# Left operands 64 bytes off x's places, second matrix all decoded in the first product's stage, attention's tail planned by arrival

## The chip, the cores and the metric

The kernel runs on one core of a Trainium2 chip. Its time is device time in microseconds. Places in time are measured from the start of the profiled span.

## What is computed

Softcapped attention without a mask, then a two-layer block with a squared ReLU. Only the lines that compute are kept:

```python
# q, k, v: (4, 12, 448, 64) float32; w_in: (768, 2048), w_out: (2048, 768) as 64-bit floats
scores = cap * np.tanh(np.matmul(q, k.transpose(0, 1, 3, 2)) / np.sqrt(64) / cap)
attn = np.exp(scores - scores.max(-1, keepdims=True))
attn = attn / (attn.sum(-1, keepdims=True) + 1e-09)
x = np.matmul(attn, v).transpose(0, 2, 1, 3).reshape(1792, 768)
h = np.maximum(x @ w_in, 0.0)
return (h * h @ w_out).astype(np.float32)
```

The two matrices come as 64-bit floats, so the kernel fetches their raw words and turns them into 32-bit values itself. This is called decoding here.

## The kernel before

The core works in three stages.

**Attention**, about 0 to 177 us. 24 pairs of heads (`n`), one iteration of the loop each (`for n in range(NP + 1)`). PE does the scores (L389, L397), ACT the tanh and the exponential (L407, L415), PE the sums (L440) and the product with v (L431, L434, L447). DVE transposes q and k, adds, copies the two results out of PSUM (`take_sums`, `evac`), inverts the sums (`invert`, L464 and L465) and multiplies (`normalise`, L487). Between `invert` and `normalise` the reciprocals go to DRAM and come back spread over the partitions, by two DMAs that POOL issues (`spread`, L475). Six halves of `w_in` are decoded in the gaps.

**First product**, about 177 to 390 us: x @ w_in by Strassen's scheme. x is kept as four blocks `x11`, `x12`, `x21`, `x22`, and each block and each left operand is split in a high and a low part, so that one product is three matmuls for each of three chunks (L337). Four units with the blocks themselves ("u") come first, then seven products of two times nine matmuls for each pair `p` of 128 columns of w_in (`seq`, L664). Sums of blocks, `t1` to `t4` (`minus`, L742; `t1` = `x12` − `x11`), and their splits (`split_x`: ACT's high part L717, DVE's low part L723) are made at the beginning of this stage. Left operands come from decoded halves of `w_in` (`round_pair`, `other_ops`, `split_w`), and the results go through ReLU to `g_dram`. In the same stage halves of `w_out` are decoded (`part`) and stored to `w_dram`. A half costs ACT two steps (L39, L42) and DVE four (L40, L43, L45, L47).

The order of this stage is written by a planner (`Plan`). Each task has an engine, a cost, what it comes after with a lag, a due time, at times an earliest start (`ready`) and a buffer token. The planner goes through time, gives each engine the task that can start first and, among those, the one due first, and emits the instructions in that order. On the chip each engine then works through its queue in this order and waits where something has not arrived. The planner's time 0 is some 173 us of the span, and its `END` is 204.5. A half of `w_out` may not be fetched more than 16 before its due time (`round_half(..., early)`), and the due times lie evenly between `WSTART` and `END - WEND`.

**Second product**, 390 us to the end: relu² @ w_out, also by Strassen, in 49 products of 24 matmuls (L1096) in the order of `PRODUCTS`. The loop variable `z` counts them. In step z the raw `a` for product z + 5 is loaded from `g_dram` (L992) and the one of z + 4 squared on ACT (L996). The left operand of product z + 2 is split into `gh` (ACT, L1085) and `gl` (DVE, L1086), and `weights(z)` makes the right operands `th`, `tl`, two 1536-column halves at a time (L1180, L1184, L1185). Three pairs of buffers hold left operands, two in the pool `opp` on the right side of SBUF and one in `opp2` on the left. In this stage before the change the last eight halves of `w_out` are fetched and decoded in steps 0 to 8 (`fetch_half`, `round_half_to`).

**Places in SBUF.** Pools are laid one after another from the left (`lctx`, `rctx`, `actx`, `mctx`) and from the right. A pool that is opened over closed ones waits until those are done with as a whole, unless it has `reuse_waits="tile"`. In the layout of the kernel before, the pools `xab`, `w` (tiles `op`), `xf`, `xg0`, `xg1`, `xg2` all begin 32 bytes past a multiple of 128, and all their tiles are multiples of 128 long. In the second product `th` and `tl` lie at 32; `gh` and `gl` lie at 96, in `opp2` because of the pool `opad` (48 words) in front of it, and in `opp` because the right-hand end of the space lies at 96. `opp2` lies over `ep`, where the tiles `u`, `e`, `es`, `rb` were, and `scr` and `scr2`, with the decode's tiles, are on the right.

Of the kernel before, what the change touches and what calls it, by code (L numbers as in the profile page):

```python
# [239 lines left out]
def tile_softcap_attention_mlp(ctx, tc, q, k, v, cap, w_in, w_out, out):  # L240
# [18 lines left out]
    NRAW = 7  # L259
    LEAD = 5  # L260
    WSTART, WEND = 65.0, 15.0
# [7 lines left out]
    sctx = ctx.enter_context(ExitStack())  # L269
    actx = ctx.enter_context(ExitStack())  # L270
    xab = lctx.enter_context(tc.tile_pool(name="xab", bufs=NQ))
    wpool = rctx.enter_context(tc.tile_pool(name="w", bufs=8))
    xf = rctx.enter_context(tc.tile_pool(name="xf", bufs=2 * NQ))
    tmp = rctx.enter_context(tc.tile_pool(name="tmp", bufs=3))
    ep = rctx.enter_context(tc.tile_pool(name="ep", bufs=2))
    ps_s = rctx.enter_context(tc.tile_pool(name="ps_s", bufs=3, space=PSUM))

    hpad = actx.enter_context(tc.tile_pool(name="hpad", bufs=1))
    hpad.tile([P, 112], F32, name="hpad")
    qp = actx.enter_context(tc.tile_pool(name="qp", bufs=4))  # L280
    scr = sctx.enter_context(tc.tile_pool(name="scr", bufs=1, side="right"))
# [30 lines left out]
    def fetch_w(pool, f, o, first, bufs, tag="wraw"):  # L312
        raw = pool.tile([P, HO], U64, tag=tag, name="wraw", bufs=bufs)
# [182 lines left out]

    E = mybir.EngineType
# [76 lines left out]
    for n in range(NP + 1):  # L574
# [50 lines left out]
        if old:  # L625
            evac(n - 1)

    make_identity(nc, ident)
    for _ in decoding:
# [8 lines left out]
    xg = [c.enter_context(tc.tile_pool(name=f"xg{i}", bufs=NHALF, reuse_waits="tile"))  # L638
          for i, c in enumerate((rctx, tctx, tctx))]
    scr2 = sctx.enter_context(tc.tile_pool(name="scr2", bufs=1, side="right", reuse_waits="tile"))  # L640
# [211 lines left out]
    t1 = [minus(at + c, x11[c], x12[c], x11[c]) for c in range(NHALF)]  # L852
# [125 lines left out]
    quads = [(f, o) for o in range(2) for f in range(NF) if f < HF or not o]  # L978
# [11 lines left out]
    def load_a(tt, k):  # L990
        t = later["raw"].tile([P, HF, P], F32, tag="a", name="a")
# [29 lines left out]
    def move():  # L1021
        tctx.close()
        sctx.close()
        for name, bufs in (("opp", 2), ("raw", NRAW), ("tb", 2)):
            later[name] = lctx.enter_context(tc.tile_pool(name=name, bufs=bufs, side="right", reuse_waits="tile"))
# [3 lines left out]
    b21 = [None, None]  # L1029

    def load_b21(g):
        b21[g] = later["tb"].tile([P, HG * HO], F32, tag="t", name="tr")
        nc.sync.dma_start(out=b21[g], in_=w_dram[1, 0, g])

# [26 lines left out]
    for g in range(2):  # L1061
        do("SP", 0.35, partial(load_b21, g), moved, *stores[1, 0], lag=6.0, due=END - 8.0 + g)
# [4 lines left out]
    with ExitStack() as mctx:  # L1067
        mctx.enter_context(tc.manual_schedule(engines={E.PE, E.Activation, E.DVE, E.SP}))
        ps_o2 = mctx.enter_context(tc.tile_pool(name="ps_o2", bufs=6, space=PSUM))
        tw2 = mctx.enter_context(tc.tile_pool(name="tw2", bufs=12))  # L1070
        mctx.enter_context(tc.tile_pool(name="opad", bufs=1)).tile([P, 48], F32, name="opad")
        opp2 = mctx.enter_context(tc.tile_pool(name="opp2", bufs=1))
        ob = mctx.enter_context(tc.tile_pool(name="ob", bufs=3))
        sv = mctx.enter_context(tc.tile_pool(name="sv", bufs=2 * HT))
# [86 lines left out]
        def fetch_t():  # L1161
            tr[0] = [new_t(tw2, F32) for _ in range(2)]
            for g in range(2):
                nc.sync.dma_start(out=tr[0][g], in_=w_dram[0, 1, g])

        halves = {}

        def fetch_half(k):
            if k == 0:
# [106 lines left out]
```

## Time and profile before

| | us |
|---|---|
| median of 3 runs | 607.47 |
| lowest, highest | 606.35, 607.81 |
| the profiled execution, its own time | 608.97 |
| its span, first to last instruction | 607.40 |
| PE busy in the span | 586.2 |
| attention / first product / second product, about | 177 / 213 / 213 |

The profile is one execution. Its table by stage gives the busy time of each engine in each stretch, the granted clock of PE as a share of 2.4 GHz, the mean busy share of the DMA engines, and GB/s. The timeline gives start, length, engine and line, and in brackets how long the engine had stood idle before it and what released it. "x36" stands for 36 instructions in a row. Matmuls overlap, so a run of n matmuls is measured from its start to the start of the next run.

### The profile page before, as it was taken

To read this page: it belongs to the slowest core of one execution; us is meant where nothing else is said; L and a number is where in the kernel's file an instruction comes from. 1 tells how busy PE (TensorE), PEld (TensorE's weight loads), DVE (VectorE), ACT (ScalarE), POOL (GpSimd) and SP (SyncE) were. 2 spreads that over 40 slices of the span, in tenths; PEclk is the share of its full clock that TensorE was granted. 3 is DMA by queue.
4 is the path that set the end of the run, shared out by engine and by line. 5 is a ranking of instruction groups with operands and counts; after the bars stand their busy time and mean duration, and the time that the engine had idled before them with its cause. 6 is when DMAs were issued, how large, how long until landed. Compare 5 with 4: busy or idle time off the path is not lost. (4 is left out here: it accounts for less than half of the span.)

```text
span 607.4 us, 9533 instructions
## 1 busy us (share of the span) xinstructions
PE 586.2 (97%) x3286; PEld 459.2 (76%) x3286; DVE 488.4 (80%) x787; ACT 418.8 (69%) x564; POOL 125.3 (21%) x197
## 2 busy tenths in 40 slices
PE   8999999999999899999999999979999999999996
PEld 5333333333368789999989999869999899999996
DVE  2879999999868998898988885349999998766751
ACT  5998889999953676676767665659778965454430
POOL 8687788775310000000000000000000000000000
PEclk9999999999999999999999999989999999999999
DMA  9999797595424316788776885978599616656611
GB/s 132 140 169 173 142 161 149 129 161 125 104 53 135 114 56 210 218 259 250 239 240 206 250 257 195 339 258 262 163 260 307 187 36 196 190 159 167 178 39 43
DMA packets 149270, 107.04 MB, mean 176 GB/s; under 512 B 54528, under 2 KB 139776, under 8 KB 149216
## 3 DMA queue, kind: packets, MB, share of 16 engines
q1 hardware_dynamic: 140032, 89.69, 55.3%
q0 software_dynamic: 7648, 16.41, 13.7%
q8 instruction: 27, 0.44, 0.3%
q10 hardware_dynamic: 1536, 0.27, 0.3%
q14 instruction: 27, 0.22, 0.2%
HBM read 81.27 MB, written 24.99 MB: 175 GB/s over the span
## 5 line engine op out<-in xcount | busy, mean ns | idle before, releaser
L1096 PE MATMUL po<-th,gh 128*128 128x384 f32 x728 | 190.6, 337 | 4.0 <-ACT gh L1085 4.0
L1096 PEld LDWEIGHTS po<-th,gh 128*128 128x128 f32 x728 | 132.5, 189 | 4.4 <-ACT gh L1085 4.4
L1096 PE MATMUL po<-th,gl 128*128 128x384 f32 x392 | 132.6, 338 | 1.8 <-DVE gl L1086 1.8
L337 PE MATMUL hps<-xt,op 128*128 128x448 f32 x450 | 94.7, 367 | 0.3 <-DVE xt L723 0.3
L1085 ACT CAST gh<-a 128x1024 fp32r<-128x1024 f32 x47 | 49.3, 1048 | 61.5 <-PE po L1096 46.1
L337 PEld LDWEIGHTS hps<-xt,op 128*128 128x128 f32 x450 | 84.3, 188 | 8.2 <-DVE xt L723 0.7
L407 ACT ACTIVATE p<-sc 128x896 f32<-128x896 f32 x84 | 73.1, 909 | 17.4 <-PE sc L389 17.3
L1096 PEld LDWEIGHTS po<-th,gl 128*128 128x128 f32 x392 | 74.1, 189 | 3.1 <-DVE gl L1086 3.1
L415 ACT ACTIVATE p<-p 128x1792 f32<-128x1792 f32 (+1 forms) x48 | 72.5, 1510 | 1.3
L337 PE MATMUL hps<-xs,op 128*128 128x448 f32 x324 | 69.4, 368 | 2.7 <-ACT hps L932 2.7
L1086 DVE TENSOR_TENSOR gl<-a,gh 128x1024 fp32r<-128x1024 f32 x47 | 57.3, 1219 | 14.0 <-ACT gh L1085 14.0
L337 PEld LDWEIGHTS hps<-xs,op 128*128 128x128 f32 x324 | 60.3, 188 | 10.5 <-ACT hps L932 4.0
L996 ACT ACTIVATE a<-a 128x1024 f32<-128x1024 f32 x56 | 57.9, 1054 | 9.3 <-DMA a<-g_dram 9.1
L389 PE MATMUL sc<-kq 64*128 64x448 f32 x288 | 60.7, 554 | 0.0
L447 PE MATMUL pa<-p,vn 128*64 128x448 f32 x288 | 59.4, 548 | 0.0
L346 POOL DMA_DIRECT2D kqn<-in_k_dram x92 | 58.6, 643 | 3.6 <-issue 1.7
L337 PE MATMUL hps<-xh,op 128*128 128x448 f32 x168 | 50.5, 367 | 1.2 <-ACT u L942 1.2
L389 PEld LDWEIGHTS sc<-kq 64*128 64x128 f32 x288 | 25.7, 186 | 34.0 <-issue 24.1
L42 ACT ACTIVATE rest<-wraw 128x384 uint32<-128x384 uint32 x64 | 35.3, 552 | 10.6 <-DVE wf L47 10.6
L447 PEld LDWEIGHTS pa<-p,vn 128*64 128x64 f32 x288 | 18.5, 136 | 30.9 <-issue 30.9
L371 POOL DMA_DIRECT2D vn<-in_v_dram x48 | 35.3, 740 | 31.9 <-PE pa L447 23.6
L47 DVE CUSTOM_DVE_ANT_0 wf<-wf,rest 128x768 uint16<-128x768 uint16 x56 | 30.9, 552 | 6.8 <-ACT rest L42 2.3
(95 smaller groups left out, 839.2 us busy)
## 6 DMA issues: line engine op xcount, KB each, us to landing
a<-g_dram SPq DMA_DIRECT2D x56, 512.0 KB
wraw<-in_moe_w_in_dram SPq DMA_DIRECT2D x32, 384.0 KB
wraw<-in_moe_w_out_dram SPq DMA_DIRECT2D x32, 384.0 KB
g_dram<-r SPq DMA_DIRECT2D x36, 224.0 KB
g_dram<-u SPq DMA_DIRECT2D x28, 224.0 KB
vn<-in_v_dram POOLq DMA_DIRECT2D x48, 112.0 KB, 4.6
rb<-rd POOLq DMA_DIRECT2D x48, 112.0 KB, 3.5
kqn<-in_q_dram SPq DMA_DIRECT2D x93, 56.0 KB
```

What stands on the lines that cost most here:

```text
L42: rest=lambda rest: nc.scalar.activation(out=rest, in_=low, func=ACTF.Copy, scale=2.0 ** -29),
L337: nc.tensor.matmul(out=out, lhsT=w, rhs=x[:, j], start=start and c == 0 and s == 0, stop=stop and c == NHALF - 1 and s == 2, skip_group_ch ...
L346: queue.dma_start(out=kqn[n % NKQ][32 * a:32 * a + 32, i], in_=x)
L371: nc.gpsimd.dma_start(out=vn[n % NKV][r, at:at + NS], in_=x[i::2].rearrange("t r d -> r t d"))
L389: nc.tensor.matmul(out=sc[:, h, :S], lhsT=kt[r, keys(n, h, u)], rhs=qt[r], start=True, stop=True)
L407: nc.scalar.activation(out=p, in_=probs[n, u][:, :, :S], func=ACTF.Tanh, scale=by["qks"])
L415: nc.scalar.activation(out=p, in_=p, func=ACTF.Exp, scale=by["cap"])
L447: nc.tensor.matmul(out=pvs[n, 0][r], lhsT=vn[n % NKV][:, v_slot(n, h, u)], rhs=p[:, h], start=False, stop=(u == NU - 1))
L996: nc.scalar.activation(out=x, in_=x, func=ACTF.Square)
L1085: last["act"] = nc.scalar.copy(out=hi, in_=x)
L1086: last["dve"] = nc.vector.tensor_sub(out=lo, in0=x, in1=f32(hi))
L1096: last["mm"] = nc.tensor.matmul(out=po, lhsT=w[:, c], rhs=m[:, cols], start=(c == 0 and i == 0), stop=(c == HF - 1 and i == 2))
```

## The change

- Pads of 16 words before and behind the pool `w` and of 24 and 8 words at the right-hand end (`shift`); `xg1`, `xg2` go to the right side, `scr` and `scr2` to the left, `hpad` gets 32 words fewer.
- All 32 halves of `w_out` are decoded by `part` in the first product's stage, with due times from 85 to END + 15 instead of 24 halves from 65 to END − 15. `fetch_half` and `round_half_to` are gone; the loop of the second product loads decoded halves from `w_dram` (`fetch_t`), `b21` among them, which the planner loaded before. `opp2` and `tw2` (now 14 tiles) come to lie over `scr` as well.
- The raw `a` tiles are in six buffers on the right and one on the left.
- `t1` is made in attention, in five of its six parts (`t1_part`, at iterations 17, 18, 19, 23, 24); the sixth is planned.
- The plan for the last two reciprocals: later `ready` times, longer lags, and `spread_b` no longer behind `spread_a`.
- `moved`, which opens the pools for the second product's operands, waits for products 5 and 6 alone.

```diff
-    NRAW = 7
+    NRAW = 6
-    WSTART, WEND = 65.0, 15.0
+    WSTART, WEND = 85.0, -15.0
...
+    def shift(stack, name, words, **kw):
+        stack.enter_context(tc.tile_pool(name=name, bufs=1, **kw)).tile([P, words], F32, name=name)
+    shift(rctx, "pad1", 16)
     wpool = rctx.enter_context(tc.tile_pool(name="w", bufs=8))
+    shift(rctx, "pad2", 16)
     xf = rctx.enter_context(tc.tile_pool(name="xf", bufs=2 * NQ))
...
+    scr = rctx.enter_context(tc.tile_pool(name="scr", bufs=1))
-    hpad.tile([P, 112], F32, name="hpad")
+    hpad.tile([P, 80], F32, name="hpad")
-    scr = sctx.enter_context(tc.tile_pool(name="scr", bufs=1, side="right"))
...
+    def t1_part(c, j):
+        x, y = x_of(0, 0, c)[:, j], x_of(1, 0, c)[:, j]
+        nc.vector.tensor_sub(out=x, in0=y, in1=x)
...
         if old:
             evac(n - 1)
+        for j, at in enumerate((2 * NPAIR + 5, 3 * NPAIR + 5)):
+            if 0 <= n - at < NHALF:
+                t1_part(n - at, j)
...
-    xg = [c.enter_context(tc.tile_pool(name=f"xg{i}", bufs=NHALF, reuse_waits="tile"))
-          for i, c in enumerate((rctx, tctx, tctx))]
-    scr2 = sctx.enter_context(tc.tile_pool(name="scr2", bufs=1, side="right", reuse_waits="tile"))
+    shift(tctx, "pad3", 24, side="right", **by_tile)
+    xg = [c.enter_context(tc.tile_pool(name=f"xg{i}", bufs=NHALF, **by_tile, **kw))
+          for i, (c, kw) in enumerate(((rctx, {}), (tctx, dict(side="right")), (tctx, dict(side="right"))))]
+    scr2 = rctx.enter_context(tc.tile_pool(name="scr2", bufs=1, **by_tile))
...
-    spread_a = do("POOL", 0.7, lambda: spread(NP - 2), lag=3.4)
-    invert_b = do("DVE", 0.6, lambda: invert(NP - 1), ready=6.2, lag=2.3)
-    spread_b = do("POOL", 0.7, lambda: spread(NP - 1), spread_a, invert_b, lag=3.4)
+    spread_a = do("POOL", 0.7, lambda: spread(NP - 2), ready=4.0, lag=6.5)
+    invert_b = do("DVE", 0.6, lambda: invert(NP - 1), ready=6.5, lag=2.5)
+    spread_b = do("POOL", 0.7, lambda: spread(NP - 1), invert_b, lag=4.5)
...
-    t1 = [minus(at + c, x11[c], x12[c], x11[c]) for c in range(NHALF)]
+    t1 = [None] * (NHALF - 1) + [do("DVE", 0.62, lambda: t1_part(NHALF - 1, 1), due=at)]
...
-    quads = [(f, o) for o in range(2) for f in range(NF) if f < HF or not o]
+    quads = [(f, o) for o in range(2) for f in range(NF)]
...
-        t = later["raw"].tile([P, HF, P], F32, tag="a", name="a")
+        pools = [later[name] for name in ["raw"] * NRAW + ["raw2"] if name in later]
+        t = turn(n_raw, *pools).tile([P, HF, P], F32, tag="a", name="a")
...
-        for name, bufs in (("opp", 2), ("raw", NRAW), ("tb", 2)):
-    moved = when(*[t for ts in stores.values() for t in ts], *[o.lo for o in left_ops.values()], *users[6, NFP - 1],
-                 *users[5, NFP - 1], emit=move)
-    for g in range(2):
-        do("SP", 0.35, partial(load_b21, g), moved, *stores[1, 0], lag=6.0, due=END - 8.0 + g)
+        shift(lctx, "pad4", 8, side="right", **by_tile)
+        for name, bufs in (("opp", 2), ("raw", NRAW)):
+    moved = when(*users[6, NFP - 1], *users[5, NFP - 1], emit=move)
...
-        tw2 = mctx.enter_context(tc.tile_pool(name="tw2", bufs=12))
+        tw2 = mctx.enter_context(tc.tile_pool(name="tw2", bufs=14))
+        later["raw2"] = mctx.enter_context(tc.tile_pool(name="raw2", bufs=1))
...
-            if k in (0, 1):
-                split_half(2, b21, tw2, k)
+            if k in (2, 3):
+                split_half(2, b21, tw2, k - 2)
...
-            if z == 2:
-                fetch_t()
-            if z < HF:
-                fetch_half(z)
+            if z == 0:
+                b21 = fetch_t(1, 0)
+            if z in (2, 4):
+                tr[z // 2 - 1] = fetch_t(z // 2 - 1, 1)
-            if 0 < z <= HF:
-                round_half_to(z - 1)
```

## Rows read from the trace of the kernel before

**Rows 1.** The page, part 1: busy us (share of span) xinstructions.

```profile
PE 586.2 (97%) x3286; PEld 459.2 (76%) x3286; DVE 488.4 (80%) x787; ACT 418.8 (69%) x564; POOL 125.3 (21%) x197
```

**Rows 2.** Table by stage: stretch, its us, busy per engine, PEclk, DMA share, GB/s.

```profile
177.00:185.00 8.00, 8.00 (x41) 7.30 (x40) 2.12 (x5) 4.09 (x8) 1.19 (x2) 1.00 0.67 155
...
250.00:300.00 50.00, 50.00 (x248) 46.20 (x248) 45.04 (x100) 36.21 (x77) 0.00 (x0) 1.00 0.82 248
300.00:350.00 50.00, 49.23 (x240) 44.65 (x239) 42.90 (x96) 34.80 (x74) 0.00 (x0) 1.00 0.75 231
350.00:377.00 27.00, 27.00 (x133) 24.51 (x132) 21.52 (x42) 17.92 (x34) 0.00 (x0) 1.00 0.70 231
377.00:390.30 13.30, 12.06 (x58) 10.45 (x57) 2.47 (x3) 6.40 (x10) 0.00 (x0) 1.00 1.07 307
...
440.00:475.00 35.00, 35.00 (x204) 35.00 (x203) 35.00 (x34) 27.93 (x27) 0.00 (x0) 1.00 1.07 280
```

**Rows 3.** Timeline of PE in the first product: start us, us, engine line.

```profile
213.08 7.46 PE L337 MATMUL hps<-xt,op 128*128 128x448 f32 x36
220.38 0.36 PE L337 MATMUL hps<-xh,op 128*128 128x448 f32 x1
...
318.07 7.60 PE L337 MATMUL hps<-xt,op 128*128 128x448 f32 x36
325.51 0.37 PE L337 MATMUL hps<-xh,op 128*128 128x448 f32 x1
```

**Rows 4.** The chain that ended last, its longest piece: start us, us, what.

```profile
498.90 103.94 PE po L1096 x598
```

**Rows 5.** Timeline from attention's end to 226 us, all engines, in order of time.

```profile
184.26 0.63 DVE L487 TENSOR_TENSOR xf<-e,rb 128x448 f32<-128x448 f32 x1 [5.78 <-DMA rb<-rd]
...
185.80 0.22 DVE L464 TENSOR_SCALAR cmp<-cmp,guard 32x28 f32<-32x28 f32 x1
...
187.72 0.38 SPq L315 DMA_DIRECT2D wraw<-in_moe_w_in_dram  x1
...
191.38 0.55 ACT L39 ACTIVATE wf<-wraw 128x384 f32<-128x384 f32 x1 [2.45 <-DMA wraw<-in_moe_w_in_dram]
...
195.52 7.97 PE L337 MATMUL hps<-xt,op 128*128 128x448 f32 x38 [0.28 <-DVE xt L723]
...
221.91 0.47 PE L337 MATMUL hps<-xl,op 128*128 128x448 f32 x1 [0.56 <-DVE xl L723]
...
225.52 3.81 PE L337 MATMUL hps<-xs,op 128*128 128x448 f32 x18
```

**Rows 6.** Groups by line, whole span: xcount, busy us, mean ns of one.

```profile
L45 DVE SCALAR_TENSOR_TENSOR wf<-wraw,wf 128x384 uint32<-128x384 uint32 x56 | 30.9, 554 | 1.4
...
L43 DVE TENSOR_SCALAR wf<-wf 128x384 uint32<-128x384 uint32 x56 | 19.7, 352 | 1.4
...
L487 DVE TENSOR_TENSOR xf<-e,rb 128x448 f32<-128x448 f32 x24 | 14.8, 615 | 5.8 <-DMA rb<-rd 5.8
...
L742 DVE TENSOR_TENSOR xf<-xf 128x896 f32<-128x896 f32 x11 | 11.7, 1082 | 0.0
```

**Rows 7.** Timeline of the seam between the two products, SP's queue, ACT and PE.

```profile
382.36 2.08 SPq L1033 DMA_DIRECT2D tr<-w_dram  x2
...
390.38 0.34 PE L1096 MATMUL po<-th,gh 128*128 128x384 f32 x1
...
394.27 1.51 SPq L678 DMA_DIRECT2D g_dram<-u  x1
...
401.81 1.04 ACT L1085 CAST gh<-a 128x1024 fp32r<-128x1024 f32 x1 [7.63 <-DMA g_dram<-u]
...
402.91 0.65 PE L1096 MATMUL po<-th,gh 128*128 128x384 f32 x1 [4.04 <-ACT gh L1085]
...
406.50 0.33 PE L1096 MATMUL po<-th,gh 128*128 128x384 f32 x1
```

**Rows 8.** Timeline of PE in the second product, its longest later wait.

```profile
481.75 0.44 PE L1096 MATMUL po<-th,gl 128*128 128x384 f32 x1 [1.30 <-DVE gl L1086]
```

**Rows 9.** Table by stage, iteration 17 of attention; columns as in rows 2.

```profile
125.00:131.30 6.30, 6.30 (x44) 2.22 (x43) 6.13 (x11) 5.62 (x7) 4.89 (x9) 1.00 1.21 187
```

More of the change, by code (lines that the diff above doesn't have):

```diff
@@ L268, in tile_softcap_attention_mlp @@
     rctx = ctx.enter_context(ExitStack())
-    sctx = ctx.enter_context(ExitStack())
     actx = ctx.enter_context(ExitStack())
     xab = lctx.enter_context(tc.tile_pool(name="xab", bufs=NQ))
+    def shift(stack, name, words, **kw):
+        stack.enter_context(tc.tile_pool(name=name, bufs=1, **kw)).tile([P, words], F32, name=name)
+    shift(rctx, "pad1", 16)
     wpool = rctx.enter_context(tc.tile_pool(name="w", bufs=8))
+    shift(rctx, "pad2", 16)
     xf = rctx.enter_context(tc.tile_pool(name="xf", bufs=2 * NQ))
@@ L310, in tile_softcap_attention_mlp, with fetch_w @@
     xs, xt = {}, {}
-    def fetch_w(pool, f, o, first, bufs, tag="wraw"):
-        raw = pool.tile([P, HO], U64, tag=tag, name="wraw", bufs=bufs)
+    def fetch_w(pool, f, o, first, bufs):
+        raw = pool.tile([P, HO], U64, tag="wraw", name="wraw", bufs=bufs)
         if first:
@@ L637, in tile_softcap_attention_mlp @@
     tctx = ctx.enter_context(ExitStack())
-    xg = [c.enter_context(tc.tile_pool(name=f"xg{i}", bufs=NHALF, reuse_waits="tile"))
-          for i, c in enumerate((rctx, tctx, tctx))]
-    scr2 = sctx.enter_context(tc.tile_pool(name="scr2", bufs=1, side="right", reuse_waits="tile"))
+    by_tile = dict(reuse_waits="tile")
+    shift(tctx, "pad3", 24, side="right", **by_tile)
+    xg = [c.enter_context(tc.tile_pool(name=f"xg{i}", bufs=NHALF, **by_tile, **kw))
+          for i, (c, kw) in enumerate(((rctx, {}), (tctx, dict(side="right")), (tctx, dict(side="right"))))]
+    scr2 = rctx.enter_context(tc.tile_pool(name="scr2", bufs=1, **by_tile))
     ps_o = lctx.enter_context(tc.tile_pool(name="ps_o", bufs=2, space=PSUM, side="right"))
@@ L1022, in move @@
         tctx.close()
-        sctx.close()
-        for name, bufs in (("opp", 2), ("raw", NRAW), ("tb", 2)):
-            later[name] = lctx.enter_context(tc.tile_pool(name=name, bufs=bufs, side="right", reuse_waits="tile"))
-    moved = when(*[t for ts in stores.values() for t in ts], *[o.lo for o in left_ops.values()], *users[6, NFP - 1],
-                 *users[5, NFP - 1], emit=move)
[L1029 to L1033, printed above, removed]
+        shift(lctx, "pad4", 8, side="right", **by_tile)
+        for name, bufs in (("opp", 2), ("raw", NRAW)):
+            later[name] = lctx.enter_context(tc.tile_pool(name=name, bufs=bufs, side="right", **by_tile))
+    moved = when(*users[6, NFP - 1], *users[5, NFP - 1], emit=move)
     ops2 = {}
@@ L1159, in finish, with fetch_t @@
                 put(i + HT, 0, s7[i], po, sub)
-        def fetch_t():
-            tr[0] = [new_t(tw2, F32) for _ in range(2)]
+        def fetch_t(k, o):
+            ts = [new_t(tw2, F32) for _ in range(2)]
             for g in range(2):
[L1164 to L1169, printed above, removed]
-                tr[1] = [new_t(tw2, F32) for _ in range(2)]
-            halves[k] = fetch_w(later["raw"], HF + k, HO, False, NRAW, "a")
-        def round_half_to(k):
-            g, c = divmod(k, HG)
-            rest = ob.tile([P, HO], U32, tag="osb", name="rest")
-            for _ in decode(nc, halves.pop(k), tr[1][g][:, c * HO:(c + 1) * HO], rest):
-                pass
+                nc.sync.dma_start(out=ts[g], in_=w_dram[k, o, g])
+            return ts
         def combine_half(op, out, x, y, g):
```

## Prediction

> **What bounds the kernel now.** I read the page's engine line first: PE is busy 586.2 of the 607.4 us [rows 1], so every gain is either a shorter distance between two matmuls or one of the few places where PE stands still. Then the table by stage shows where another engine is as full as PE [rows 2]: DVE has 5.0 us free of 50 at 250 to 300 us, 7.1 at 300 to 350, none at 440 to 475, but 5.9 of 8 at 177 to 185, 5.5 of 27 at 350 to 377 and 10.8 of 13.3 at 377 to 390. Last I followed PE through the timeline. Three things are to be seen there.
>
> First, the pace. In the first product 36 matmuls of 448 columns take 7.30 us from 213.08 (203 ns each), but 7.44 us from 318.07 (207 ns) [rows 3]; I counted some 690 at the first pace and 320, in one run from 314 to 381 us, at the second. 448 columns at 2.4 GHz are 186.7 ns, so 16 and 20 ns lie on top. In the second product 598 matmuls of 384 columns take 103.94 us with two short waits among them, 173.8 ns [rows 4]; without the waits I count 173.3, which is 160.0 plus 13.3 ns, at one pace all through. Second, the seam at attention's end: DVE stands 5.78 us until 184.26 for the spread reciprocals, everything behind it is late, and PE pays at 195.5 and 221.9 us [rows 5]. Third, the seam between the products, with 4.04 us of idle PE, and a late wait for DVE at 481.75 [rows 7, 8].
>
> **The change part by part.** The sum is made against the profiled execution, 608.97 us with a span of 607.40; that execution is 1.5 us above the median, 607.47, and I take the differences from the median.
>
> *Places in SBUF.* As the pools of the kernel before are sized, `op` tiles and all x tiles of the first product begin at the same remainder of 128 bytes (32), while in the second product `gh`, `gl` (96) stand 64 bytes off `th`, `tl` (32). That is the one difference between the stages that fits an overhead of 13.3 ns in one and 16 to 20 in the other. The pads put `op` at 96 with x in `xab`, `xf` and `xg0` still at 32. If those get the 13.3 ns, a matmul takes 200.0: 690 × 2.7 + 320 × 6.7 = 4.0 us less. But by the same arithmetic `pad3` of 96 bytes leaves `xg1` and `xg2` at 0, 32 bytes from `op`, not 64; they feed products 5 and 6 and four of the units, 288 of 1008 matmuls, or 1.1 us of the 4.0. No row shows a distance of 32. I take −3.5, between −2.9 and −4.0. `pad4` likewise moves the pool `opp` from 96 to 64, 32 off, for two of three products of the second stage. I take 0, as the pace has room on both sides of nothing: at the first stage's worst overhead (20 against 13.3 ns) 784 matmuls would lose 5.2 us, at its better one 2.1.
>
> The trace has two paces at one and the same pair of places, and the pace changes behind a stop of PE at 313 us. So place alone doesn't set it. The Trainium skill speaks against this part: its page SBUF — State Buffer, section "Who interferes with whom", gives TensorE two independent read ports, one for the moving operand and one for weights, and says that it never waits on anyone; by that rule the pads move nothing and this term is 0. No run here has yet shown that rule at work, and the two paces don't follow from it.
>
> *Second matrix decoded in the first product's stage.* Eight more halves go through DVE there: two steps (L40, L43) of 0.352 and two (L45, L47) of 0.554 us each [rows 6], 1.81 us a half, 14.5 in all; ACT gets 8 × 1.1. Three subtractions of 1.08 [rows 6] leave the stage and one of 0.62 stays: −2.6. So DVE gains 11.9 us of work against 16.3 idle at 350 to 390 alone [rows 2]. But the halves come due every (204.5 + 15 − 85)/32 = 4.2 us instead of 5.2, and at 250 to 350 I count 18 of them before; 24 after would take 10.5 of the 12.1 us that DVE has free. They have late due times, so the planner puts them behind what PE waits for; I take +0.7, between −0.5 and +10.5 (all of it on PE's path).
>
> In exchange the second stage loses 14.5 us of DVE work in its first eight products. At 481.75 PE waits for `gl` in the middle of 35 us in which DVE had no pause [rows 2, 8]; taken together the waits at 475 to 499 are 2.2 us. With some 4 us of DVE backlog less at product 10 they go: −2.2, at worst 0. What is late next there is the square, whose loads arrive at 1.07 of the DMA engines' share [rows 2].
>
> *The seam between the products.* `gh` of product 2 waits at 401.81 until the last store of `u` has landed, since `opp2` is opened over `ep` as a whole [rows 7]. That is E + 11.4 us, with E = 390.38 the second product's start. PE has two products to do (8.3 us), idles to 402.91 and comes back slowly, waiting for `gl` and with matmuls that take 0.65 us at first and 0.33 at 406.50: 6.2 us lost by then. After the change 3.4 MB of loads (both halves of `b21`, two `wraw`, two `a`) no longer go ahead of that store. But `opp2` and `tw2` now lie over `scr`, so they also wait for the last decoded half, and its fetch is barred until 16 us ahead of a due time of END + 15, about E − 1. A fetch to its first step takes 3.7 us when it is quiet (issued at 187.72, used at 191.38) [rows 5], and 7.5 us is what the last store needed in the backlog [rows 7]. So the region is free at E − 1 + 3.7 to 7.5, + 2.9 for the chain of the decode, + 3.7 to 7.5: E + 9.3 to E + 16.9. With a backlog that ends by then, 5.0 and 3.7: E + 10.6. I take −0.8, between −2.1 and +5.5. The load of `b21` now stands at the head of SP's queue until that moment, and behind it the fifth `a`, which ACT squares ahead of `gh` of product 4: 2.1 MB at 307 GB/s [rows 2] are 6.8 us, and PE comes to product 4 at about 11 us, so this is covered, with some 2 us to spare.
>
> *Attention's tail.* With `invert_b` planned ahead of the wait, it runs near 179.7 instead of 185.8 us [rows 5], its spread follows some 5 us earlier, and DVE uses the 5.8 us. PE's loss at 195.5 (0.45 us), in product 7 (1.5: 5.14 us from 220.38 to 225.52 against 18 × 0.203) [rows 3, 5] and part of the first wait for the seed go. I take −2.1, between −0.5 and −2.7.
>
> *Five parts of t1 in attention.* Each is one subtraction as L487, 0.615 us [rows 6]. Three land at iterations 17 to 19, where DVE is at its fullest busy 6.13 of 6.30 us while PE is never idle [rows 9]; two near 171 to 178 us, where DVE waits anyway. I take +0.4, between 0 and +1.5. POOL's and SP's queues are passed by none of them.
>
> **Sum.** −3.5 + 0.7 − 2.2 − 0.8 − 2.1 + 0.4 = −7.5 us: 607.5 − 7.5 = **600.0 us** (601.5 for an execution like the profiled one).
>
> **Rivals.** (a) The pads do not do what they say. The two paces at equal places speak for it, and the second product's one pace against it. Without the term the time is 603.5; if PE falls into 207 ns for good, another 690 × 4.0 = 2.8 us, 606.3. The 603.5 is also where that rule of the Trainium skill, page SBUF — State Buffer, leads. (b) The second product is slowed by its new distance of 32 bytes: + 2.1 to 5.2, 602.1 to 605.2. For: no clean row at 32; against: none that is bad. (c) The seam grows, as the last half is decoded behind the end of the first product: up to + 6.3 on my term, 606.3. For: END + 15; against: the loads taken out of the way. (d) **DVE becomes the bound of the first product, and the kernel slower than before.** The place is 246 to 355 us, where the four steps of eight more halves want 10.5 of 12.1 idle us. If the pauses of DVE are waits in queue order and can't be filled, each us goes to PE: 600.0 − 0.7 + 10.5 = 609.8. It turns the sign from the point where more than 8.2 us of the 10.5 fall on PE, that is, where under a fifth of the pauses can be used. Against: PE hardly waits for DVE at 225 to 390 now, and the halves' due times are late.
>
> **How the numbers follow.** The forecast with its own range 597 to 603 has 0.5; (a) 0.2, (b) 0.13, (c) 0.1, (d) 0.07. The low end adds the good ends of the terms for places, tail and seam, −4.0 − 2.7 − 2.1 − 0.5 − 2.2, with half of t1's cost: about 596; the high end takes in (a), (b) and (c): 606. A difference under 0.3% (1.8 us) can't be told from none here. Faster by more is all of the forecast and most of (a) to (c): 0.81. Same: the upper parts of (a) and (c) and the mild end of (d): 0.11. Slower: (d) in earnest, or (b) and (c) together: 0.08.
>
> **What would show it.** Places: matmuls of products 1, 2, 3, 4 and 7 at 200 ns, those of 5 and 6 perhaps not; a first product at 203 or 207 falls to (a). Second product: 173.3 ns whatever buffer holds the left operand; a pace that alternates over three products is (b). Seam: `gh` of product 2 at E + 10.6, released by a store of `w_dram` rather than of `u`. Decode: 32 stores of `w_dram`, DVE over 95% busy at 250 to 350 without new idle PE. Tail: no DVE wait of 5.8 us, and products 7 of p = 1 in 3.65 us. Late: no PE wait for `gl` at products 19 to 24. I am wrong most cheaply if the seam goes past E + 13, most dearly if left operands of the first product come late.

## The result, and the profile after

The changed kernel takes 614.65 us (median of 4; 613.35 to 614.96) against 607.64 for the kernel before in the same session: **1.14% slower**, ratio 1.0114, interval 1.0092 to 1.0136, or 7.0 us. The forecast was 600.0 with a range of 596 to 606. Sign and range are both wrong. The profiled execution has a span of 613.1 us against 607.4 [rows 1], which is 5.7 us and not 7.0, as the profiled execution of the kernel before was itself 1.3 us above the median of 607.64. In the kernel after the lines are numbered anew (L343 is the matmul of the first product, L1104 of the second, L801 and L804 make the halves of a left operand, L1021 loads `b11`, L990 stores a decoded half).

By the starts of the matmuls in both traces, the last matmul comes 5.9 us later. These are made up so:

| us | before | after | difference | forecast |
|---|---|---|---|---|
| first product, pace of its matmuls | 204.0 ns | 202.3 ns | −1.7 | −3.5 |
| first product, stops of PE at 187 to 245 us | 4.7 | 4.8 | +0.1 | −1.7 (tail and t1) |
| stops at 245 to 355 us | 1.1 | 0 | −1.1 | +0.7, with the next row |
| stop at 367.5 us, half clock behind it | 0 | 6.6 | +6.6 | |
| products 0 to 2 of the second stage, above 173.3 ns | 6.2 | 7.5 | +1.3 | −0.8 |
| late waits at 475 to 499 us | 2.2 | 0 | −2.2 | −2.2 |
| wait for the operand of product 4 | 0 | 0.5 | +0.5 | 0 |
| second product from product 3 on, pace | 173.3 ns | 173.3 and 176.7 ns | +2.4 | 0 |

The forecast failed most at the stop at 367.5 us, at the pace of the second product, and at products 0 to 2, which are called the seam here. The first product's pace and its early stops each gave 1.8 us less than forecast. The stop and the paces are seen in the timeline of PE in the kernel after (start, length, line, operation, count; in brackets the idle time before and what ended it):

```profile
258.51 3.76 PE L343 MATMUL hps<-xt,op 128*128 128x448 f32 x18
262.11 3.81 PE L343 MATMUL hps<-xs,op 128*128 128x448 f32 x18
265.76 7.52 PE L343 MATMUL hps<-xt,op 128*128 128x448 f32 x36
273.12 0.37 PE L343 MATMUL hps<-xh,op 128*128 128x448 f32 x1
...
371.44 10.33 PE L343 MATMUL hps<-xt,op 128*128 128x448 f32 x36 [3.63 <-ACT op L801]
381.61 0.36 PE L343 MATMUL hps<-xh,op 128*128 128x448 f32 x1
...
511.69 0.51 PE L1104 MATMUL po<-th,gh 128*128 128x384 f32 x2
515.85 0.52 PE L1104 MATMUL po<-th,gh 128*128 128x384 f32 x2
520.09 0.52 PE L1104 MATMUL po<-th,gh 128*128 128x384 f32 x2
524.33 0.51 PE L1104 MATMUL po<-th,gh 128*128 128x384 f32 x2
```

From one start to the next: product 3 has 3.60/18 = 200.0 ns, product 2 202.8, products 6 and 5 7.36/36 = 204.4. At 371.44 the same two products of the last pair take 10.2 us instead of 7.4, after 3.63 us of standing still for a left operand. (The same pair of products has more than one pace: for some pairs `p` they take 7.43 us, 206.4 ns.) In the second product one product takes 4.16 us (173.3 ns), then two take 4.24 (176.7). The table by stage shows what happened at 367:

```profile
core 0: us, PE busy (x) PEld busy (x) DVE busy (x) ACT busy (x) POOL busy (x), PEclk, DMA share, GB/s
300.00:350.00 50.00, 50.00 (x250) 46.37 (x249) 45.42 (x101) 37.41 (x78) 0.00 (x0) 1.00 0.85 267
360.00:365.00 5.00, 5.00 (x26) 4.67 (x25) 2.68 (x7) 2.88 (x6) 0.00 (x0) 1.00 0.98 337
365.00:378.00 13.00, 9.37 (x33) 8.14 (x33) 9.08 (x18) 7.76 (x13) 0.00 (x0) 0.74 0.80 265
```

At 300 to 350 us DVE is busy 45.4 of 50 us (42.9 before [rows 2]) and PE never stands. At 360 to 365, just ahead of the stop, DVE stands idle 2.3 of 5 us and ACT 2.1, and the DMA engines are full, 0.98. In 365 to 378 PE's granted clock is 0.74: 14 matmuls of 448 columns lie 0.372 us apart, which is 1.2 GHz.

### The profile page after: what moved, and what is told of

It is laid out like the page before. It is cut to its first block, busy times and chain, and to the rows that moved or that the text cites. A ratio compares the mean times of both kernels' runs of the same rounds, so it can differ in the third digit from the quotient of the medians.

```text
span 613.1 us, 9550 instructions
## 1 busy us (share of the span) xinstructions
PE 588.8 (96%) x3286; PEld 463.2 (76%) x3286; DVE 488.8 (80%) x790; ACT 419.8 (68%) x564; POOL 125.2 (20%) x197
## 4 chain that ended last, share of the span: by engine, by line
PE 59%; DMA 3%; DVE 3%; ACT 2%; issue 1%; SPq 0%; DVEq 0%; ACTq 0%
PE po L1104 31%; PE hps L343 28%; DMA w_dram<-wf 1%; DMA a<-g_dram 1%; DMA g_dram<-u 1%; DVE wf L47 0%; DVE wf L45 0%; DVE xt L738 0%; ACT r L701 0%; DVE wf L43 0%; ACT th L1025 0%; ACT op L801 0%; DVE wf L40 0%; DVE gl L1094 0%; DVE wf L809 0%
## 5 line engine op out<-in xcount | busy, mean ns | idle before, releaser
L1104 PE MATMUL po<-th,gh 128*128 128x384 f32 x728 | 192.0, 339 | 5.1 <-ACT gh L1093 5.1
L1104 PEld LDWEIGHTS po<-th,gh 128*128 128x128 f32 x728 | 133.1, 188 | 5.4 <-ACT gh L1093 5.4
L1104 PE MATMUL po<-th,gl 128*128 128x384 f32 x392 | 133.1, 340 | 0.6 <-DVE gl L1094 0.6
L343 PE MATMUL hps<-xt,op 128*128 128x448 f32 x450 | 97.6, 374 | 4.9 <-ACT op L801 4.7
L343 PEld LDWEIGHTS hps<-xt,op 128*128 128x128 f32 x450 | 86.4, 193 | 14.0 <-ACT op L801 5.4
L1104 PEld LDWEIGHTS po<-th,gl 128*128 128x128 f32 x392 | 74.0, 189 | 1.4 <-DVE gl L1094 1.4
L343 PE MATMUL hps<-xs,op 128*128 128x448 f32 x324 | 68.8, 366 | 1.8 <-ACT hps L947 1.8
L343 PEld LDWEIGHTS hps<-xs,op 128*128 128x128 f32 x324 | 60.3, 188 | 8.8 <-ACT hps L947 2.8
L343 PE MATMUL hps<-xh,op 128*128 128x448 f32 x168 | 49.9, 364 | 1.2 <-ACT u L957 1.2
L39 ACT ACTIVATE wf<-wraw 128x384 f32<-128x384 f32 x64 | 35.1, 550 | 15.9 <-DMA wraw<-in_moe_w_in_dram 4.8
L42 ACT ACTIVATE rest<-wraw 128x384 uint32<-128x384 uint32 x64 | 35.3, 552 | 12.4 <-DVE wf L47 12.0
```

The source lines that it names most:

```text
L42: rest=lambda rest: nc.scalar.activation(out=rest, in_=low, func=ACTF.Copy, scale=2.0 ** -29),
L343: nc.tensor.matmul(out=out, lhsT=w, rhs=x[:, j], start=start and c == 0 and s == 0, stop=stop and c == NHALF - 1 and s == 2, skip_group_ch ...
L1104: last["mm"] = nc.tensor.matmul(out=po, lhsT=w[:, c], rhs=m[:, cols], start=(c == 0 and i == 0), stop=(c == HF - 1 and i == 2))
```

## Experiments

The ratios are to runs of the kernel before on the same chip in the same session; where the text gives a ratio in microseconds, it is taken of 607.64. The other columns are read from one profiled execution each: us, and for the pace ns a matmul. "Stop" is the time that PE loses around products 2 and 6 of the last pair, half clock included; "seam" is what products 0 to 2 of the second stage take above 173.3 ns a matmul; "late" what products 3 to 48 do. The first product runs from its first matmul to the second product's first.

| kernel | ratio (95% interval) | first product | pace | stop | seam | late |
|---|---|---|---|---|---|---|
| before | 1 | 220.98 | 204.0 | 0 | 6.23 | 2.21 |
| after | 1.0114 (1.0092, 1.0136) | 224.81 | 202.3 | 6.6 | 7.48 | 2.95 |
| a_places64 | 1.0036 (1.0018, 1.0054) | 223.20 | 200.9 | 7.0 | 8.93 | 0.00 |
| b_pads_alone | 0.9971 (0.9956, 0.9986) | 218.32 | 200.8 | 0 | 8.16 | 0.73 |
| c_no_decode_move | 0.9939 (0.9917, 0.9961) | 215.64 | 200.9 | 0 | 6.94 | 1.50 |
| d_old_dates | 1.0352 (1.0326, 1.0379) | 245.86 | 202.0 | four | 0.16 | 2.40 |
| e_less_dve | 0.9991 (0.9974, 1.0008) | 222.74 | 200.9 | 6.2 | 6.09 | 0.05 |
| f_more_dve | 0.9966 (0.9950, 0.9982) | 217.21 | 200.8 | 0 | 7.51 | 1.01 |
| g_tail_alone | 1.0006 (0.9990, 1.0021) | 220.14 | 203.4 | 0 | 7.45 | 0.89 |
| h_t1_alone | 1.0027 (1.0005, 1.0049) | 222.81 | 204.1 | 0 | 7.85 | 0.73 |
| i_late_tr | 1.0000 (0.9983, 1.0017) | 221.09 | 200.9 | 4.5 | 7.99 | 0.00 |
| j_early_fetch | 1.0088 (1.0071, 1.0105) | 226.08 | 200.8 | 8.4 | 6.81 | 0.37 |
| k_both_earlier | 0.9937 (0.9906, 0.9968) | 217.86 | 200.9 | 0.3 | 5.96 | 0.03 |
| l_later_a | 0.9916 (0.9892, 0.9940) | 217.90 | 200.8 | 0.3 | 6.92 | 0.00 |
| m_other_side | one execution, 607.44 us | 218.85 | 200.1 | 0 | 7.96 | 0.79 |

Seven of these kernels (before, b, c, f, g, h, m) have the same second product, and in their traces the seam still goes from 6.2 to 8.2 us and "late" from 0.7 to 2.2. A difference of that size between two rows shows nothing by itself.

### Places: a, b and m

```diff
 # a_places64, on the kernel after
-    shift(tctx, "pad3", 24, side="right", **by_tile)
+    shift(tctx, "pad3", 16, side="right", **by_tile)
-        shift(lctx, "pad4", 8, side="right", **by_tile)
 # b_pads_alone, on the kernel before; m_other_side has 48 and 48 for pad1 and hpad
+    shift(rctx, "pad1", 16)
+    shift(rctx, "pad2", 16)
-    hpad.tile([P, 112], F32, name="hpad")
+    hpad.tile([P, 80], F32, name="hpad")
```

> The changed kernel with pad3 at 64 bytes instead of 96 and pad4 left out, so that every left operand of both products lies 64 bytes off its right operand's place; nothing else differs. Theory 1 (the pace hangs on the distance of the two operands): products 5 and 6 go from 204 to 207 ns to between 200 and 202.5, that is 252 matmuls by some 4 ns or 1.0 us; the second product has 173.3 ns at all 49 products instead of 176.65 at 33 of them, 33 x 24 x 3.3 = 2.6 us; the time falls by 3.6 from 614.6 to 611.0 (609.8 to 612.0), still slower than before. Rival (the paces are states that PE falls into at a stop, as at 313 us of the kernel before, whatever the places): the two paces of the second product and those of products 5 and 6 stay, 614.6 within 1.

> The kernel before with pad1 and pad2 alone (64 bytes each, and hpad shorter by the same 128 bytes, so that all else stays where it was): op 64 bytes off every x tile of the first product; the second product's places unchanged. Theory 1 (distance sets the pace): all of the first product at 200 to 202.5 ns where the kernel before had 202.6 and 206.7 in two stretches; 1008 matmuls by about 2.9 ns, so 2.9 us less: 604.7 (603.7 to 605.7). Rival (the pads do nothing, the pace is a state that a stop of PE sets): 607.6, or up to 610.4 if the 207 ns pace holds all through.

> b_pads_alone with pad1 at 192 bytes instead of 64, so that op lies 64 bytes below the x tiles of xab by address modulo 256, as it does for those of xf and xg, instead of 64 above. Theory 1a (the side counts modulo 256, not the distance alone): products 1 and 2 and the first units, which read xab, go from 201.7 to 202.5 ns down to 200.0, as all others are; 324 matmuls by 2 ns, 0.7 us, which only the pace in the trace can show: 606 (604.5 to 607.5). Rival 1b (the 2 ns belong to the tiles of xab for another reason, their separate buffers for the two halves say): 202 ns stays, 606.5.

`a_places64` is 0.78% below the kernel after, 4.7 us (3.6 expected; 3.5 between the last matmuls of the two traces), and the second product is at 173.3 ns throughout. `b_pads_alone` gains 1.8 us in time; its first product is 2.7 us shorter, and its seam, which has the same code as before, was 1.9 us longer in that execution. `m_other_side` in the timeline of PE:

```profile
237.43 3.77 PE L344 MATMUL hps<-xs,op 128*128 128x448 f32 x18
241.03 7.62 PE L344 MATMUL hps<-xt,op 128*128 128x448 f32 x36
```

Product 2, which reads `xab` (`xs`), takes 3.60 us here, 200.0 ns, against 202.8 in the kernel after. In m the two places lie 64 bytes the other way round modulo 256, so the distance counts with its sign. Left operand less right operand, modulo 256, as worked out from the sizes of the pools, gives in the first product

- −64: 200.0 ns, in every kernel that has it;
- +64: 201.7 to 202.8 ns;
- −32: 204.4 or 206.7 ns in the kernel after, but 200.0 in two products of `d_old_dates`, at 332.0 and 399.2 us, which follow stops of PE;
- 0: 202.6 or 206.7 ns (before, g, h);

and in the second product −64 gives 173.3 ns and −96 gives 176.7. The rival of a pace set by PE's stops falls for ±64. For 0 and −32, place alone doesn't set the pace; what else does stays open. The forecast's use of the Trainium skill, page SBUF — State Buffer, section "Who interferes with whom" (PE has two independent read ports and never waits on anyone, so the pads move nothing), isn't borne out: product 2 costs 202.8 ns at one place and 200.0 at another.

### What the move of the decode costs: c, d, e, f

```diff
 # c_no_decode_move: before + pad1, pad2, hpad as in b + new dates of spread_a, invert_b, spread_b + t1_part
 # d_old_dates, on the kernel after
-    WSTART, WEND = 85.0, -15.0
+    WSTART, WEND = 65.0, 15.0
 # e_less_dve, on a_places64, for halves of the second matrix (first is False)
-        clip = do("DVE", 0.36, lambda: h.steps.clip(), ...
+        clip = do("DVE", 0.36, lambda: h.steps.clip() if first else None, ...
-        shift = do("DVE", 0.36, lambda: h.steps.shift(), ...
+        shift = do("DVE", 0.36, lambda: h.steps.shift() if first else None, ...
 # f_more_dve, on c_no_decode_move
-        clip = do("DVE", 0.36, lambda: h.steps.clip(), ...
+        clip = do("DVE", 0.36, lambda: [h.steps.clip() for _ in range(1 if first else 2)], ...
```

> The changed kernel without the move of the second matrix: the kernel before with pad1 and pad2, the new plan of attention's tail and the five early parts of t1; 24 halves decoded in the first product's stage and 8 in the second, dates, queues and pools as before. Theory A (the loss comes from the move of the eight halves, with the two wrong places that its pools brought): places -2.9, tail -2.1, parts of t1 +0.4, so 607.6 - 4.6 = 603.0 (601.5 to 604.5), and the move with its pools is worth +11.6. Rival B (the new tail plan or the parts of t1 carry the loss, by the stops of PE at 194.6, 207.0 and 210.2 us): 608 or more, and the move costs under 6.

> The changed kernel with the dates of the second matrix's halves as in the kernel before (65 us to END - 15 instead of 85 to END + 15), still all 32 of them in the first product's stage. Theory A (two separate prices: halves ahead of the last pair's left operands in the engines' order, and the last halves behind the end of the first product): the stores of w_dram end ahead of the second product's start E, gh of product 2 is no longer released by them and PE's gap there falls from 5.4 to about 4 us (-1.5 or better), while the halves come every 3.9 us instead of 4.2, so the stops in the first product stay, some +4 us against the kernel before: 613 (611 to 615). Rival D (the bound is DVE's room in the middle of the stage): the denser halves cost more there than the seam gives back: 616 or more. Rival E (the late dates alone made the loss, since they let the last halves crowd the last pair): the stop at 367 us goes too, and the time falls to 607 or less.

> The changed kernel with the places mended (a_places64), and in it the steps L40 and L43 of DVE left out for the 32 halves of the second matrix, so those halves are not decoded to the right values; the order of all other instructions, buffers, fetches and stores is the same. It takes 32 x 0.71 = 22.7 us of work from DVE's queue and nothing from any other engine. Theory D (the move made DVE's queue the bound of the first product): the stop of 4.7 us ahead of product 6 of the last pair goes with the half clock behind it (2.8 us), and the wait between the products falls too: 610.5 - 7.5 = 603 or less (599 to 604). Rival R (the bound is room: three raw and four wf buffers handed round between the two matrices, and fetches that arrive late): the stop stays at 3 us or more, 608 to 611.

> The kernel without the move (c_no_decode_move), with step L40 of DVE issued twice for each of the 24 halves of the second matrix that it decodes in the first product's stage (the second one changes no value): 24 x 0.37 = 8.9 us more work on DVE, which is what the move added there (208.7 against 199.8 us busy), but no more fetches, buffers or ACT work, and the order unchanged. Theory D (DVE's queue is the bound once it has some 9 us more to do): 604.3 + 4 to + 9, 608 to 613, with stops of PE ahead of products 6. Rival R (room and fetches): DVE's pauses take it in, 604.3 to 606.

`c` says where the loss lies: without the move, the pads, the tail and t1 are together worth −0.6%, and the move, with its places mended (a against c), costs 0.97%, 5.9 us. `e`, which leaves out two steps of the decode, and `f`, which adds one, then ask whether the amount of DVE's work is the cause, and both say no. The first product's row in the table by stage (columns as above), of a, c, e and f:

```profile
169.13:392.34 223.21, 214.67 (x1057) 194.93 (x1056) 188.17 (x378) 146.97 (x290) 4.40 (x8) 0.98 0.67 205
```

```profile
170.03:385.66 215.63, 211.94 (x1056) 193.03 (x1055) 180.26 (x359) 142.25 (x281) 4.40 (x8) 1.00 0.67 205
```

```profile
169.17:391.92 222.75, 214.19 (x1057) 194.19 (x1055) 169.07 (x320) 145.42 (x290) 4.40 (x8) 0.99 0.67 207
```

```profile
169.11:386.32 217.21, 212.38 (x1056) 192.91 (x1055) 187.80 (x383) 143.18 (x281) 4.41 (x8) 1.00 0.66 203
```

With as much DVE work as a (187.8 against 188.2 us), f has no stop, and its first product is 6.0 us shorter than that of a and 1.6 longer than that of c; with 19.1 us of DVE work less than a, e keeps the stop:

```profile
370.21 9.26 PE L343 MATMUL hps<-xt,op 128*128 128x448 f32 x36 [4.10 <-ACT op L801]
```

So rival (d) of the forecast, DVE's work as the bound, has the right sign and not the mechanism of this stop. What `e` gains, 0.45%, lies mostly at the seam in the two traces, where the last halves are decoded (8.93 to 6.09 us). `d` went the way of its rival D in time, with 21 us more and PE waiting 17.9 us for left operands at four pairs,

```profile
PE hps L343 <- ACT op L801: 17.9, 4, 8.0
```

but it did not test DVE by itself: denser dates also mean more fetches, stores and buffers in the same time. Of the chains of work that end in its four stops, the first goes through a store (3.15 us) and the last through a fetch of `w_out` (8.22 us); the other two go through steps of DVE and ACT alone. Its seam is 0.16 us, as the last half's store was issued 21 us before the second product; the stops cost many times what that gives.

### Which wait makes the stop: i, j, k

The timeline of ACT and SP in the kernel after, ahead of the stop (SPq rows are issues of DMAs):

```profile
357.48 0.87 SPq L1021 DMA_DIRECT2D tr<-w_dram  x2
358.44 1.40 SPq L326 DMA_DIRECT2D wraw<-in_moe_w_out_dram  x2
...
361.59 0.41 SPq L990 DMA_DIRECT2D w_dram<-wf  x1
362.10 0.39 SPq L326 DMA_DIRECT2D wraw<-in_moe_w_out_dram  x1
...
366.07 0.54 ACT L39 ACTIVATE wf<-wraw 128x384 f32<-128x384 f32 x1 [2.52 <-DMA wraw<-in_moe_w_out_dram]
...
368.16 0.56 ACT L39 ACTIVATE wf<-wraw 128x384 f32<-128x384 f32 x1 [0.63 <-DMA w_dram<-wf]
368.62 1.46 ACT L1025 CAST th<-tr 128x1536 fp32r<-128x1536 f32 x1
...
370.88 0.51 ACT L801 CAST op<-wf 128x384 fp32r<-128x384 f32 x1
```

The two loads of `b11` (`tr`, 768 KB each) go out at 357.48, and behind them on SP fetches of `w_out` and the store of a decoded half. ACT comes to a `w_out` half that PE needs only in the second product, waits 2.52 us for its fetch, then for the store that frees a `wf` buffer, and makes the operand of product 6 (L801) at 370.88 behind them. In the chain of work that ends in the stop, the store is the longest piece beside PE's own work. Here it is in the kernel after, then in a_places64:

```profile
361.59 6.55 DMA w_dram<-wf
```

```profile
359.45 7.25 DMA w_dram<-wf
```

The chains of e and j have it too, with 7.04 and 7.61 us. It is a store of 192 KB; two such stores at the seams of k and l took 1.87 and 2.04. The Trainium skill, page DMA: Bandwidth & Descriptors, section "Queues, rings and completion order", says that on each DMA engine the descriptors of an issuing queue are consumed in order; the trace fits that, since SP had issued 1.5 MB of `b11` and two fetches of 384 KB just ahead of the store. The loads of `b11` alone don't make the stop: c issues them at 355.90 us, with a store at 359.89 behind them, and ACT waits for no DMA there between 350 and 385 us.

```diff
 # i_late_tr, on a_places64
-  loads.append(do("SP", 0.35, partial(load_b11, g), *stores[0, 0], lag=6.0, due=END - 30.0 + g, ...
+  loads.append(do("SP", 0.35, partial(load_b11, g), *stores[0, 0], lag=6.0, ready=END - 18.0, due=END - 30.0 + g, ...
 # j_early_fetch, on a_places64
-        h = round_half(False, f, o, at, 16.0)
+        h = round_half(False, f, o, at, 24.0)
 # k_both_earlier: i and j, and
-    WSTART, WEND = 85.0, -15.0
+    WSTART, WEND = 75.0, -15.0
```

> The changed kernel with the places mended (a_places64) and the two loads of b11 (tr, 768 KB each, issued at 355.5 us there, when the last pair's and the second matrix's halves are being fetched and stored) barred until 18 us ahead of END by the plan's clock; nothing else is changed, though the plan sets the order anew from there. Theory Q (the stop ahead of product 6 of the last pair is a matter of transfers: behind the loads of b11 the fetch of a w_out half takes 8 us and the store of a wf 7.25 us, and ACT and DVE, which take their work in the written order, stand there with the last pair's operands behind them): the stop falls from 4.7 us to 2 or less, the half clock behind it goes: 610.5 - 6 = 604.5 (602.5 to 606). Rival P (it is the written order itself: in the plan's own dates PE has a stop of 2.0 us there with this edit, 1.5 without): the stop stays at 3 us or more, 608.5 to 611.

> The changed kernel with the places mended (a_places64) and the fetches of the second matrix's halves allowed 24 us ahead of their due time instead of 16; the loads of b11 as they were. In the plan's own dates the stop ahead of product 6 of the last pair falls from 1.5 to 0.8 us. Theory Q (transfers behind the loads of b11): those loads still come at 355 us, the stop stays at 3 us or more: 609 to 611. Rival P (written order, too late a fetch): the stop falls to 1.5 us or less, without half clock: 603 to 606.

> The changed kernel with the places mended, the loads of b11 barred until END - 18, fetches allowed 24 us ahead, and the halves dated from 75 us on instead of 85, ending at END + 15 as before; in the plan's own dates the first product then has no stop at the last pair and the last store of w_dram ends 3.8 us earlier against the end of the first product. Theory Q: no stop at product 6 of the last pair (-7.3 us against a_places64) and a seam that loses 7 instead of 8.9 us: 610.5 - 9 = 601.5 (600 to 603.5), faster than every kernel so far. Rival S (what the first product gains the seam gives back, since the last halves are bound by the transfers): the second product's third operand stays at the date it had, the seam loses 11 or more: 605 to 608.

`i` gave some two fifths of what theory Q wanted: the stop fell from 7.0 to 4.5 us. Its rows, then those of j and of k, all PE's timeline:

```profile
368.45 0.68 PE L343 MATMUL hps<-xt,op 128*128 128x448 f32 x2 [2.11 <-ACT op L801]
369.64 8.39 PE L343 MATMUL hps<-xt,op 128*128 128x448 f32 x34 [0.50 <-DVE op L804]
```

```profile
369.23 5.88 PE L343 MATMUL hps<-xs,op 128*128 128x448 f32 x18 [4.62 <-ACT hps L947]
376.14 7.67 PE L343 MATMUL hps<-xt,op 128*128 128x448 f32 x36 [1.03 <-ACT op L801]
```

```profile
366.62 7.63 PE L343 MATMUL hps<-xt,op 128*128 128x448 f32 x36
```

In i ACT waits for no DMA between 350 and 372 us, so the transfers are out of the way. What is left is a chain through DVE, which works from 362.73 to 369.58 without a pause. These are pieces of it:

```profile
363.27 0.36 DVE wf L40
...
368.56 0.56 DVE wf L45
369.12 0.48 DVE op L804
```

Seven steps in this stretch, 3.1 us, decode halves of `w_out` that PE needs only in the second product, and the operand that PE waits for (L804) stands behind them. So this part of the stop is the written order itself, as rival P had it. By their numbers neither theory came true: PE stands 2.6 us in i, where Q wanted 2 or less and P 3 or more.

`j` shows the transfers. In the planner's own dates it made things better (its stop 0.8 us instead of 1.5); on the chip the stop grew and moved to product 2, which waits for its seed (L947). ACT in j:

```profile
367.65 0.54 ACT L39 ACTIVATE wf<-wraw 128x384 f32<-128x384 f32 x1 [4.34 <-DMA w_dram<-wf]
368.10 1.08 ACT L947 COPY hps<-hps 128x448 f32<-128x448 f32 x2
```

It is the same wait, on the store behind the loads of `b11`, with another victim behind it in ACT's queue. So the wait in the kernel after, a, e and j comes from the transfers, and who suffers from the written order; with that wait gone, the order still costs what i shows. Neither edit alone takes the stop away; with both, and the halves dated 10 us earlier, `k` has 0.3 us of it left, and the time is 3.8 us below the kernel before. Which of k's three edits is needed wasn't taken apart: the earlier dates were not run by themselves.

### The seam: l

```diff
 # l_later_a, on k_both_earlier
-        t = do("SP", 0.35, load, moved, lag=4.5, due=END - 12.0 + i, take="a")
+        t = do("SP", 0.35, load, moved, lag=4.5, ready=(END - 6.0 + 2.0 * i) * (i > 1), due=END - 12.0 + i, take="a")
```

> k_both_earlier with the loads of a for products 2 to 4 barred until END - 2, END and END + 2 (there all five were issued from 376.1 us on, 8.2 us of SP's queue, with the stores of u and the fetch of the last w_out half behind them). Theory S2 (between the products PE waits for the last decoded half, whose fetch stands behind the loads of a): the fetch leaves some 5 us earlier, the last store of w_dram lands by E + 7 instead of E + 10.6, and the loss between the products falls from 6.0 to 3 to 4.5 us: 604.4 - 2 = 602.4 (601 to 603.5). Rival T (the squares of a for products 3 and 4 stand ahead of gh of product 2 in ACT's order, so what leaves later is waited for just as long): 604 to 606, with ACT waiting for a instead.

Rival T came true. The chain of work in l goes through a load of `a` and ACT's square of it to the last decoded half and its store:

```profile
387.11 7.14 DMA a<-g_dram
394.24 0.02 issue
394.27 1.06 ACT a L1012
395.33 0.44 ACT rest L42
...
396.38 2.04 DMA w_dram<-wf
```

ACT waits for `a` with the last half's step (L42) behind it. The third operand starts 10.7 us after the second product, as in k, and the seam is no shorter (6.9 and 6.0 us). The time of l, 0.9916, can't be told from that of c and k. The three are the fastest kernels of this study, each clearly below both the kernel before and the kernel after.

### Attention's tail and t1: g and h

`g_tail_alone` has only the new lines of `spread_a`, `invert_b` and `spread_b`, `h_t1_alone` only `t1_part` and its calls, both on the kernel before.

> The kernel before with the new plan of attention's tail alone (dates and lags of spread_a, invert_b and spread_b). The forecast's theory: DVE's wait of 5.8 us goes, and the stops of PE at 195 and 220 to 225 us with it: 607.6 - 2.1 = 605.5 (605 to 607). Rival: the wait moves to another place, as the stop at 237 to 239 us of the two runs with the new plan says (1.8 us there): 607 to 608.

> The kernel before with five of the six parts of t1 in attention's iterations alone. The forecast's theory: attention ends later by some 0.4 us and the first product's stage has 2.6 us less of DVE at 216 to 222 us: 607.6 within 1 (607.0 to 608.6). Rival: the 2.6 us come off the stops of PE at 220 to 225 us, which wait for just this chain: 606.0 to 606.8.

In g the wait of 5.78 us [rows 5] is gone, and DVE waits for ACT instead (waits of DVE, 178 to 215 us: total, times, longest):

```profile
DVE op L789 <- ACT op L786: 3.9, 2, 3.5
DVE xt L723 <- ACT xt L717: 2.8, 1, 2.8
```

PE's stops at 187 to 200 us grow from 0.55 to 1.72 us, and those at 216 to 230 fall from 1.51 to 0.60: nothing gained. In h (waits of PE, 188 to 245 us)

```profile
PE hps L337 <- ACT hps L939: 3.1, 2, 2.4
PE hps L337 <- ACT op L793: 1.0, 1, 1.0
```

the stops at 216 to 230 us go, but one of some 1.5 us comes at 237 to 244 for an operand, as in the kernel after, a, c, f and k, which also have `t1_part`, and PE's stops at 207 to 214 us double, 2.5 to 4.8 us. Together on b, though, they gave c another 0.3% (with both intervals, 0 to 0.6%). Why they help only together wasn't tried further.

## Why the prediction was wrong, step by step

The forecast had −7.5 us and the traces show +5.9 between the last matmuls. The 13.4 us between them are the decode in the first product (4.8), the second product's pace (2.4), the seam (2.1), the first product's pace (1.8), the tail with t1 (1.8) and the wait for the operand of product 4 (0.5).

**The step that decided the sign** is "They have late due times, so the planner puts them behind what PE waits for; I take +0.7". The price was +6.6 at one place, +5.5 with the 1.1 us of other stops that went. That lies inside the term's own bounds of −0.5 to +10.5, but the bounds were for another mechanism. The forecast weighed eight more halves as DVE work against DVE's free time, and DVE did have that time: f carries as much work without a stop, for 1.6 us. What had no room was the order. The dates only tell the planner what to emit first among tasks that can start; it counted 4.5 us for a fetch and 3.0 for a store, and on the chip a store took 6.55 us behind the loads of `b11` and the fetches (7.25 in a). ACT then stood, in written order, before a half that nobody needed yet. The last sentence of the forecast, "most dearly if left operands of the first product come late", names what happened, but it had no price and no chance. Rival (d) came nearest in time, 609.8; e and f refute it as the mechanism of this stop, though in i, with the transfers out of the way, steps of DVE in written order made the rest.

**Places.** The mechanism was right as far as the distances of ±64 go: 200.0 ns where the forecast had it for products 3, 4 and 7, and not for 5 and 6. It counted distances modulo 128 and without their sign, so it missed the 202 ns of products 1 and 2 at +64: the term was −1.7 and not −3.5. Mis-sized was also "I take 0" for the pool `opp`: 33 products of 24 matmuls lost 3.3 ns each, 2.6 us in full, inside the stated bound of +2.1 to +5.2. Rival (b) came true, with the pace changing over three products as described. Taking 0, outside that bound, for a layout that moved from the one good distance known to an untested one, was the error. Mended, the term is −3.1 us by pace (204.0 to 200.9 ns, 1008 matmuls) and −1.8 in b's time.

**Seam.** `gh` of product 2 was released by a store of `w_dram`, as forecast, but 12.7 us after E and not at E + 10.6. The rows of ACT after:

```profile
406.87 1.04 ACT L1093 CAST gh<-a 128x1024 fp32r<-128x1024 f32 x1 [3.30 <-DMA w_dram<-wf]
```

It lies inside the range of E + 9.3 to 16.9, so the term was mis-sized: +1.3 instead of −0.8. The +1.3 itself is no more than the seam differs between traces of one and the same code (6.2 to 8.2 us).

**Late waits.** Right in what goes: no wait for `gl` at products 19 to 24 in the kernel after, a or k. The size, −2.2, is that of one trace; other kernels that keep the eight halves there lose 0.7 to 1.5 us.

**Tail and t1.** "I take −2.1" failed: alone, the tail measures −0.6 to +1.3 us, since DVE's idle time turned into a wait for ACT. t1's +0.4 was +0.3 to +3.0 alone. In the kernel after the two gave +0.1 at PE's early stops instead of −1.7.

## What to carry to other kernels

Free time of an engine is not room in its queue: when work is put between what a critical engine waits for, look in the trace for the longest transfer that the moved steps will wait on, and price the whole wait for what stands behind it in the same queue. Change dates in a hand-written order together with the lags that the order was made from, and look at the stop again after each edit, since it changes its victim. Where operands' places set the pace, keep to a distance that the trace has shown to be good in every stage, and work out each pool's address after the change.

## What the runs showed of the hardware

For matmuls of 448 and 384 columns of 32-bit data, the pace hangs on the distance of left and right operand modulo 256 bytes, with its sign: 200.0 ns at −64 and 202 at +64 in the first product, 173.3 ns at −64 and 176.7 at −96 in the second. At −32 (200.0 to 206.7 ns) and at 0 (203 or 207) one place has several paces, and these runs don't show why.

A stop can have a second price: PE's granted clock fell to half around it (a mean of 0.74 at 365 to 378 us in the kernel after). After idle times of 3.63 us (kernel after) and 4.33 (a) PE ran its next 14 and 12 matmuls at 0.372 us, that is 1.2 GHz, 2.8 and 2.5 us more with their first ones. After 4.62 us (j) ten matmuls were at that level, after 4.10 (e) eight, after 2.11 (i) six, and after the 1.03 us at 239 us (kernel after) none, only three of 0.30 to 0.31. So a longer stop didn't always cost more.
